# A GEGLU kernel in seven-product blocks: one unit's raw products set inside the unit before it, and a third weight sum handed to GpSimd

## The chip, the cores and the metric

The kernel runs on one core of a Trainium2 chip. The metric is the device time of one execution in microseconds (us), which is less when the kernel is better. The median of four runs of the kernel before is 543.22 us (543.09 to 543.28).

## What is computed

```python
def reference(x, w_gate, w_up, w_down):
    g = jnp.einsum("bsd,df->bsf", x, w_gate)
    u = jnp.einsum("bsd,df->bsf", x, w_up)
    h = _gelu(g) * u
    return jnp.einsum("bsf,fd->bsd", h, w_down)
```

x has 2048 rows of 1024, w_gate and w_up are 1024 by 3584, w_down is 3584 by 1024, all bf16; gelu is the tanh approximation.

## The kernel before, in words

**Passes and units.** The 2048 rows go in two passes of 1024. A pass holds its rows transposed in SBUF as `xT[c]`, c = 0 and 1, each 512 rows wide and cut into eight blocks of 128 along the contraction (ko = 0 to 7). The 3584 columns of w_gate and w_up go in 14 units of 256 columns (two blocks of 128). After the units of a pass comes the down projection (`down`), which the change does not touch.

**A unit.** Except for unit 0 of pass 0, each unit computes, for gate and for up (i = 0 and 1), a 2 by 2 block product with seven block products in place of eight (Winograd's form). The weight tile gives the blocks a11, a12 (first 128 columns, lower and upper half of the contraction), a21, a22 (second 128 columns). The sums of weights (`sums_s`, L151) are s1 = a21+a22, s2 = s1-a11, s3 = a11-a21, s4 = a12-s2, and sa, which is a22 cast by ScalarE; each name stands for two instructions, one for gate and one for up. The sums of x (`sums_t`, L136) are t1, t2, t3, t4 and the cast tb, each of four instructions, made once in a pass. The sums are fp32r tiles in the slots of one pool. Each product is four matmuls of 512 columns for gate and four for up, eight in all. `unit` (L193) issues them in this order: the raw bf16 products a11 (`first_product`, L188, snapped from its banks as `p1` by ScalarE; normally issued near the end of the unit before) and a12 (L205); then s2 times t2 on top of the a11 banks; s1 times t1 (into the banks `d`, snapped as `p5`); s3 times t3; s4 times tb; the next unit's a11; sa times t4. VectorE adds the parts (`add`, L196; L230, L231, L236) and multiplies gelu by up (`times`, L181); ScalarE does the gelu and the snaps. In a steady unit each of VectorE's operations takes one operand from PSUM and one from SBUF; the sums s and t of unit 1 are made from SBUF alone.

**Who makes the sums.** From unit 2 on, GpSimd makes a unit's weight sums one unit ahead (`make_s(ahead, pool)`, L524, in `prepare`, which `unit` calls as `after_p5` at L227). For unit 1, the first in seven-product form, VectorE makes all of s1 to s4, and t1 to t4.

**The start.** Unit 0 of pass 0 is computed plainly by `plain` (L471): with ko in pairs, four banks (gate and up, two column blocks) get eight matmuls each, first for c = 0 in `bank[0:4]`, then for c = 1 in `bank[4:8]`; `finish` (L486) does gelu and `times`. The rows of c = 0 are loaded and turned by TensorE (`turn`, L441); those of c = 1 come by eight transposing DMAs, one for each ko, in SyncE's queue (L468, L448). Unit 1's weights are loaded from ScalarE's queue (L497), unit 2's from ScalarE's queue inside unit 1 (`aside(-1)`, L204 and L541), and later ones by SyncE in `prepare` (L526), as soon as one of the three buffers of the pool `w` is free.

**What sets the order.** On SyncE, VectorE, GpSimd and TensorE the order of instructions is the order of the code (`manual_schedule(engines=ORDER)`, L67). On ScalarE it is planned by the framework, except in the start block (L492 to L507), where it is the code's order too. All semaphores are set by the framework from the tiles that an instruction reads and writes. In the start block the order is: warm-up, turning, unit 1's weight load, plain c = 0, t1, finish c = 0, s1, s2, t2, t3, tb, s3, sa, plain c = 1, finish c = 1. Then unit 1 issues its a11 products, its a12 products and so on; s4 and t4 are made in `aside(0)` (L542 to L544), after s2 times t2 has been issued.

Of the kernel before, what the change touches and what calls it, by code (L numbers as in the profile page):

```python
# [1 line left out]

# [8 lines left out]
def kernel(  # L11
# [23 lines left out]
    nc = tc.nc  # L35
    ENG = mybir.EngineType
# [14 lines left out]
    NKB = Dm // P  # L51
# [43 lines left out]
    def new(eng, a, b, op, name, shape=None, dtype=None):  # L95
        t = slot(shape or [P, N], dtype or f32r, name)
        eng(t, a, b, op)
        return t
# [15 lines left out]

    def load_w(u, queue=nc.sync, pinned=False):
        f0 = u * 2 * P
        w = wpool.tile([P, 2, NKB, 2 * P], bf16, name="w")
        for i, src in enumerate((w_gate, w_up)):  # L120
            got = queue.dma_start(
                out=w[:, i],
                in_=src[:, f0 : f0 + 2 * P].rearrange("(ko ki) f -> ki ko f", ki=P),
            )
            if queue is not nc.sync and not pinned:
                tc.keep_in_program_order(got)
        return w

    class Sums(dict):
# [6 lines left out]
    def sums_t(xT):  # L136
        K = range(KH)
        lo, hi = [[xT[c][:, k] for k in K] for c in range(2)], [
            [xT[c][:, KH + k] for k in K] for c in range(2)
        ]  # L140
        return Sums(
            how={
                "t1": lambda q: [new(dve, lo[1][k], lo[0][k], SUB, "t1") for k in K],
                "t2": lambda q: [new(dve, hi[1][k], q["t1"][k], SUB, "t2") for k in K],
                "t3": lambda q: [new(dve, hi[1][k], lo[1][k], SUB, "t3") for k in K],
                "t4": lambda q: [new(dve, hi[0][k], q["t2"][k], SUB, "t4") for k in K],
                "tb": lambda q: [cast(hi[1][k], "tb") for k in K],
            }
        )

    def sums_s(w, eng):  # L151
        GU = range(2)
        sh = [P, KH, P]
        a11, a21 = [[w[:, i, :KH, h : h + P] for i in GU] for h in (0, P)]
        a12, a22 = [[w[:, i, KH:, h : h + P] for i in GU] for h in (0, P)]
        return Sums(
            how={
                "s1": lambda q: [new(eng, a21[i], a22[i], ADD, "s1", sh) for i in GU],
                "s2": lambda q: [new(eng, q["s1"][i], a11[i], SUB, "s2", sh) for i in GU],
                "s3": lambda q: [new(eng, a11[i], a21[i], SUB, "s3", sh) for i in GU],  # L160
                "s4": lambda q: [new(eng, a12[i], q["s2"][i], SUB, "s4", sh) for i in GU],
                "sa": lambda q: [cast(a22[i], "sa", sh) for i in GU],
            }
        )

    def make_t(xT):
        t = sums_t(xT)
# [16 lines left out]
    def product(ps, lhs, rhs, start):  # L184
        for k in range(KH):
            matmul(ps, lhs[:, k, :], rhs[k], start and k == 0, k == KH - 1)
# [6 lines left out]
    def unit(u, banks, xT, w, s, t, p1, after_p5, aside, keep, ahead_of_p4, snap_first):  # L193
        GU = range(2)

        def add(ps, other):  # L196

            g = new(dve, ps[0], other[0], ADD, "sum", dtype=f32)
            dve(ps[1], ps[1], other[1], ADD)
            return g, ps[1]  # L200

        b21 = [xT[0][:, KH + k, :] for k in range(KH)]
        e, c, d = banks
        aside(-1)  # L204
        for i in GU:  # L205
            product(c[i], w[:, i, KH:, :P], b21, True)
        g, up = add(c, p1)
        for i in GU:
            product(e[i], s["s2"][i], t["t2"], False)
        aside(0)  # L210
        keep(0, c[0])
        if snap_first:
            with tc.manual_schedule(engines={ENG.Activation}):
                u2 = [snap(e[i], "u2") for i in GU]
                g = gelu(g)
        else:
            g = gelu(g)
        times(2 * u, 0, g, up)
        if not snap_first:
            u2 = [snap(e[i], "u2") for i in GU]  # L220
        keep(1, c[0])
        keep(2, c[1])
        c = d
        for i in GU:
            product(c[i], s["s1"][i], t["t1"], True)
        p5 = [snap(c[i], "p5") for i in GU]
        after_p5()  # L227
        for i in GU:
            product(e[i], s["s3"][i], t["t3"], False)
        g, up = new(dve, e[0], p5[0], ADD, "sum", dtype=f32), banks[1][1]  # L230
        dve(up, e[1], p5[1], ADD)  # L231
        for i in GU:
            product(c[i], s["s4"][i], t["tb"], False)
        times(2 * u + 1, 1, gelu(g), up)
        aside(1)
        g, up = add(c, u2)  # L236
        ahead_of_p4()
        for i in GU:
            product(e[i], s["sa"][i], t["t4"], False)
        times(2 * u, 1, gelu(g), up)  # L240
        aside(2)
        times(2 * u + 1, 0, gelu(e[0]), e[1])
# [222 lines left out]
    wf = wpool.tile([P, 2, NKB, 2 * P], bf16, name="w")  # L465
    for k0, k1 in ((0, 2), (2, 5), (5, NKB)):
        load_wf(nc.sync, k0, k1)
    for ko in range(NKB):  # L468
        transposing(xT, 1, ko, N)

    def plain(ps, c, kos, parts=1):  # L471
        n = N // parts
# [15 lines left out]
            times(j, c, gelu(ps[2 * j]), ps[2 * j + 1])  # L488

    on_dve, on_act = nc.vector.tensor_copy, nc.scalar.copy  # L490
    t = sums_t(xT)
    with tc.manual_schedule(engines={ENG.Activation}):  # L492
        for _ in range(NWARM):
            nc.tensor.matmul(bank[3], lhsT=warm[:, :P], rhs=warm, start=True, stop=True)
        for i in range(NS):
            turn(xT, xn0, 0, i, on_act if i == 1 else on_dve)
        w = load_w(1, nc.scalar, pinned=True)  # L497
        s = sums_s(w, dve)
        plain(bank[0:4], 0, range(0, 2), parts=2)
        plain(bank[0:4], 0, range(2, NKB))  # L500
        t.make("t1")
        finish(bank[0:4], 0)
        s.make("s1", "s2")
        t.make("t2", "t3", "tb")
        s.make("s3", "sa")
        plain(bank[4:8], 1, range(NKB))
        finish(bank[4:8], 1)  # L507

    def making(u):
        if u < 2 or u >= NU:  # L510
            return []
        return list(range(u - 2, NJ if u == NU - 1 else u - 1))

    nxt = {}
    ahead = None
    for ip in range(NPASS):
        for u in range(1 if ip == 0 else 0, NU):
            js = making(u) if ip == 0 else []

            def prepare():  # L520
                nonlocal ahead
                nxt["w"], nxt["s"] = ahead, None
                if u + 1 < NU:
                    nxt["s"] = make_s(ahead, pool)  # L524
                if u + 2 < NU:
                    ahead = load_w(u + 2)  # L526
                if len(js) == 1:
                    store_made(js[0])
                for j in js[1:]:
                    keep_whole(j)  # L530
                if ip == 0:
                    fetch_wd(making(u + 1))

            def keep(part, ps):
                if js:
                    keep_part(js[0], part, ps)

            def aside(part):
                nonlocal ahead
                if ahead is None:  # L540
                    ahead = load_w(2, nc.scalar)  # L541
                if part == 0 and "s4" not in s:  # L542
                    s.make("s4")
                    t.make("t4")  # L544

            def ahead_of_p4():
                if u + 1 < NU:
                    nxt["p1"] = first_product(even if u % 2 else odd, xT, nxt["w"])

            e = odd if u % 2 else even  # L550
            p1 = nxt.pop("p1", None) or first_product(e, xT, w)
            unit(u, (e, cc, dd), xT, w, s, t, p1, prepare, aside, keep, ahead_of_p4, ip == 0 and u == 1)
            if u + 1 < NU:
                w, s = nxt["w"], nxt["s"]

        last = ip == NPASS - 1
        got, nxt = {}, {}

        def more(step):

            nonlocal ahead
            if last:
                return
            if step in (-1, 0, 2):
                store_made({-1: NJ - 3, 0: NJ - 2, 2: NJ - 1}[step])
            if step == 0:
                xT[:] = new_x()
            if step >= 24 and step % 2 == 0 and step // 2 - 12 < len(moves):
                c, ko = moves[step // 2 - 12]
                transposing(xT, c, ko, (2 * (ip + 1) + c) * N)  # L570
            if step == 50:
                got["w"], ahead = load_w(0), load_w(1)
            if step == 58:
                got["s"] = make_s(got["w"], dve)
            if step == 62:
                got["t"] = make_t(xT)

        down(ip, even + cc, dd + odd, last, more)
        even, odd, cc, dd = odd, even, dd, cc
        if not last:  # L580
            w, t, s = got["w"], got["t"], got["s"]
# [29 lines left out]
```

## Time and profile before

| | us |
|---|---|
| median of four runs | 543.22 |
| the profiled execution | 543.19 |
| its span | 541.1 |
| around the span | 2.1 |
| TensorE matmul busy | 534.9 (99%) |
| VectorE busy | 341.4 (63%) |
| ScalarE busy | 258.2 (48%) |
| GpSimd busy | 236.4 (44%) |
| TensorE's share of the chain that ended last | 96% |

The span is the time from the first to the last instruction in the profile of one execution. A row of the timeline merges neighbouring instructions of one group: its first number is the start, its second the busy time, xN the number of them, and the bracket the idle time before the first, with what ended it. Matmuls overlap (each row of one says 0.379 us for a bf16 matmul of 512 columns, while the next starts earlier), so a row's count and time must be read together to find how far apart they start. PE is TensorE, PEld its weight load, DVE VectorE, ACT ScalarE, POOL GpSimd, SP SyncE; SPq is SyncE's queue of DMA issues.

### The profile page before, as it was taken

To read this page: it belongs to the slowest core of one execution; us is meant where nothing else is said; L and a number is where in the kernel's file an instruction comes from. 1 tells how busy PE (TensorE), PEld (TensorE's weight loads), DVE (VectorE), ACT (ScalarE), POOL (GpSimd) and SP (SyncE) were. 2 spreads that over 40 slices of the span, in tenths; PEclk is the share of its full clock that TensorE was granted. 3 is DMA by queue.
4 is the path that set the end of the run, shared out by engine and by line. 5 is a ranking of instruction groups with operands and counts; after the bars stand their busy time and mean duration, and the time that the engine had idled before them with its cause. 6 is when DMAs were issued, how large, how long until landed. Compare 5 with 4: busy or idle time off the path is not lost.

```text
span 541.1 us, 7420 instructions
## 1 busy us (share of the span) xinstructions
PE 534.9 (99%) x2405; PEld 377.7 (70%) x2405; DVE 341.4 (63%) x526; ACT 258.2 (48%) x463; POOL 236.4 (44%) x212
## 2 busy tenths in 40 slices
PE   8999999999999999999999999999999999999997
PEld 4477777766776646888876677667777775488885
DVE  3886666676667895594945545555544459676730
ACT  2566666556665410255355555555555541114431
POOL 0069966677774400000097777777766600000000
PEclk9999999999999999999999999999999999999999
DMA  8875666666654899989772222222331069473751
GB/s 218 176 190 176 175 176 197 204 184 189 201 174 162 269 380 317 294 189 300 229 194 79 78 79 78 79 78 80 85 100 50 1 174 379 166 236 95 238 181 48
DMA packets 108133, 93.28 MB, mean 172 GB/s; under 512 B 17216, under 2 KB 92992, under 8 KB 108096
## 3 DMA queue, kind: packets, MB, share of 16 engines
q1 hardware_dynamic: 103936, 90.72, 57.6%
q10 hardware_dynamic: 4160, 2.10, 1.5%
q8 instruction: 19, 0.31, 0.2%
q14 instruction: 18, 0.15, 0.1%
HBM read 74.45 MB, written 15.20 MB: 166 GB/s over the span
## 4 chain that ended last, share of the span: by engine, by line
PE 96%; SPq 2%; DMA 2%; ACT 0%; issue 0%
PE bank L111 96%; SPq L448 2%; DMA xT<-in_x_dram 1%; DMA xn<-in_x_dram 1%; SPq L437 0%; ACT st L408 0%
## 5 line engine op out<-in xcount | busy, mean ns | idle before, releaser
L93 POOL TENSOR_TENSOR s<-w 128x512 fp32r<-128x512 bf16 x100 | 117.3, 1194 | 185.6 <-PE bank L111 155.1
L111 PE MATMUL bank<-t,s 128*128 128x512 f32 x648 | 157.0, 398 | 0.0
L111 PEld LDWEIGHTS bank<-t,s 128*128 128x128 f32 x648 | 121.7, 188 | 27.7
L111 PE MATMUL bank<-xT,w 128*128 128x512 bf16 (+1 forms) x504 | 116.6, 377 | 0.3 <-DMA xT<-in_x_dram 0.2
L107 ACT COPY p<-bank 128x512 f32<-128x512 f32 x124 | 70.3, 591 | 92.2 <-PE bank L111 92.2
L90 DVE TENSOR_TENSOR hT<-g,bank 128x512 bf16<-128x512 f32 x112 | 76.6, 687 | 54.7 <-ACT g L178 48.3
L111 PEld LDWEIGHTS <-w 128*128 128x128 bf16 x504 | 45.0, 98 | 59.9 <-issue 14.3
L90 DVE TENSOR_TENSOR sum<-bank,p 128x512 f32<-128x512 f32 x54 | 37.4, 692 | 52.9 <-PE bank L111 51.2
L178 ACT ACTIVATE g<-sum 128x512 f32<-128x512 f32 x81 | 51.5, 636 | 33.3 <-DVE sum L90 32.3
L111 PE MATMUL bank<-q 128*128 128x512 f32 x240 | 58.9, 389 | 0.0
L111 PE MATMUL bank<-t,sa 128*128 128x512 f32 x216 | 58.6, 413 | 0.0
L93 POOL TENSOR_TENSOR s<-w,s 128x512 fp32r<-128x512 bf16 x50 | 57.7, 1177 | 0.0
L93 POOL TENSOR_TENSOR s<-s,w 128x512 fp32r<-128x512 f32 x50 | 57.1, 1163 | 0.0
L111 PE MATMUL bank<-tb,s 128*128 128x512 f32 x216 | 53.3, 389 | 0.0
L111 PEld LDWEIGHTS bank<-q 128*128 128x128 f32 x240 | 45.0, 188 | 9.4
L111 PE MATMUL bank<-raw,hT 128*128 128x512 bf16 x224 | 48.7, 379 | 0.0
L111 PEld LDWEIGHTS bank<-t,sa 128*128 128x128 f32 x216 | 40.7, 188 | 10.6
L111 PEld LDWEIGHTS bank<-tb,s 128*128 128x128 f32 x216 | 40.5, 188 | 8.4
L102 ACT CAST tb<-raw 128x512 fp32r<-128x512 bf16 x28 | 17.2, 626 | 60.0 <-PE bank L111 25.5
L107 ACT COPY u<-bank 128x512 f32<-128x512 f32 x62 | 35.9, 590 | 20.2 <-PE bank L111 20.2
L90 DVE TENSOR_TENSOR bank<-bank,p 128x512 f32<-128x512 f32 x54 | 37.8, 700 | 8.3 <-PE bank L111 5.2
L90 DVE TENSOR_TENSOR q<-hT 128x512 fp32r<-128x512 bf16 x56 | 38.5, 687 | 4.6 <-PE bank L111 4.6
(44 smaller groups left out, 441.0 us busy)
## 6 DMA issues: line engine op xcount, KB each, us to landing
raw<-in_w_down_dram SPq DMA_DIRECT2D x80, 256.0 KB, 4.8
q<-td SPq DMA_DIRECT2D x60, 256.0 KB, 4.9
w<-in_w_gate_dram SPq DMA_DIRECT2D x25, 512.0 KB, 5.5
w<-in_w_up_dram SPq DMA_DIRECT2D x25, 512.0 KB, 6.6
td<-m SPq DMA_DIRECT2D x12, 768.0 KB, 4.5
w<-td SPq DMA_DIRECT2D x6, 1024.0 KB, 9.7
out_dram<-st SPq DMA_DIRECT2D x32, 128.0 KB, 1.7
td<-w SPq DMA_DIRECT2D x2, 768.0 KB, 7.0
```

Of the source, the lines that this page charges most:

```text
L90: nc.vector.tensor_tensor(out=out, in0=a, in1=b, op=op)
L93: nc.gpsimd.tensor_tensor(out=out, in0=a, in1=b, op=op)
L102: nc.scalar.copy(out=t, in_=src)
L107: nc.scalar.copy(out=t, in_=ps)
L111: nc.tensor.matmul(ps, lhsT=lhs, rhs=rhs, start=start, stop=stop, skip_group_check=True)
L178: nc.scalar.activation(g, src, ACT.Gelu_apprx_tanh)
L448: nc.sync.dma_start_transpose(out=xT[c][:, ko, :], in_=x2[r0 : r0 + N, ko * P : (ko + 1) * P])
```

## The change

Five edits, all in pass 0 around units 0 to 2.

1. Loads: unit 1's weights are loaded from SyncE's queue between the fourth and the fifth transposing DMA, unit 2's from the same queue after the eighth. No load is issued by ScalarE any more.
2. Order on TensorE: plain c = 1 is cut in two. After its first half (ko 0 to 3) come unit 1's a11 products and its a12 products, then its second half (ko 4 to 7), called from inside `unit` as `aside(-2)`.
3. Order on VectorE: t1, finish c = 0, s1, s2, t2, the sum of a12 and a11 (`add`), t3[0] and t3[1], finish c = 1, t3[2] and t3[3], s4, t4. s3 is not VectorE's any more.
4. GpSimd makes unit 1's s3: s3 of gate behind t2's last instruction, s3 of up behind t3[1]. The gate is a copy by GpSimd of one column of the tile that VectorE has just written (`pool_behind`). Unit 2's sums are gated in the same way behind t4's last instruction.
5. In unit 1 ScalarE's order is the code's order; the multiplication of the first quarter (`c11`) moves behind the sum with p5, and that sum's up part goes to the other bank of `cc`.

```diff
-    def load_w(u, queue=nc.sync, pinned=False):
+    def load_w(u, queue=nc.sync):
...
-                "t3": lambda q: [new(dve, hi[1][k], lo[1][k], SUB, "t3") for k in K],
+                "t3": lambda q, K=K: [new(dve, hi[1][k], lo[1][k], SUB, "t3") for k in K],
...
-                "s3": lambda q: [new(eng, a11[i], a21[i], SUB, "s3", sh) for i in GU],
+                "s3": lambda q, GU=GU: [new(eng, a11[i], a21[i], SUB, "s3", sh) for i in GU],
...
+    def pool_behind(tile):
+        nc.gpsimd.tensor_copy(out=seen, in_=tile[:, :1].bitcast(f32))
...
         e, c, d = banks
-        aside(-1)
         for i in GU:
             product(c[i], w[:, i, KH:, :P], b21, True)
+        aside(-2)
         g, up = add(c, p1)
+        aside(-1)
         for i in GU:
             product(e[i], s["s2"][i], t["t2"], False)
         aside(0)
         keep(0, c[0])
         if snap_first:
-            with tc.manual_schedule(engines={ENG.Activation}):
-                u2 = [snap(e[i], "u2") for i in GU]
-                g = gelu(g)
+            u2 = [snap(e[i], "u2") for i in GU]
+            g = gelu(g)
         else:
             g = gelu(g)
-        times(2 * u, 0, g, up)
+        c11 = g, up
         if not snap_first:
+            times(2 * u, 0, *c11)
             u2 = [snap(e[i], "u2") for i in GU]
...
-        g, up = new(dve, e[0], p5[0], ADD, "sum", dtype=f32), banks[1][1]
+        g, up = new(dve, e[0], p5[0], ADD, "sum", dtype=f32), banks[1][not snap_first]
         dve(up, e[1], p5[1], ADD)
+        if snap_first:
+            times(2 * u, 0, *c11)
...
-    for ko in range(NKB):
+    for ko in range(KH):
         transposing(xT, 1, ko, N)
+    w = load_w(1)
+    for ko in range(KH, NKB):
+        transposing(xT, 1, ko, N)
+    ahead = load_w(2)
...
-        w = load_w(1, nc.scalar, pinned=True)
-        s = sums_s(w, dve)
         plain(bank[0:4], 0, range(0, 2), parts=2)
         plain(bank[0:4], 0, range(2, NKB))
         t.make("t1")
         finish(bank[0:4], 0)
+        plain(bank[4:8], 1, range(KH))
         s.make("s1", "s2")
-        t.make("t2", "t3", "tb")
-        s.make("s3", "sa")
-        plain(bank[4:8], 1, range(NKB))
-        finish(bank[4:8], 1)
+        nxt = {"p1": first_product(odd, xT, w)}
+
+    seen = xpool.tile([P, 1], f32, name="seen")
+    on_pool = sums_s(w, pool)["how"]["s3"]
+
+    def rest_of_0(part):
+        if part == 0:
+            t.make("t2", "tb")
+            plain(bank[4:8], 1, range(KH, NKB))
+            pool_behind(t["t2"][-1])
+            s["s3"] = on_pool(s, range(1))
+        else:
+            t3 = t["how"]["t3"](t, range(0, 2))
+            pool_behind(t3[-1])
+            s["s3"] += on_pool(s, range(1, 2))
+            finish(bank[4:8], 1)
+            t["t3"] = t3 + t["how"]["t3"](t, range(2, KH))
+            s.make("sa")
...
             def prepare():
                 nonlocal ahead
+                if first:
+                    pool_behind(t["t4"][-1])
...
             def aside(part):
-                nonlocal ahead
-                if ahead is None:
-                    ahead = load_w(2, nc.scalar)
+                if (ip, u) == (0, 1) and part < 0:
+                    rest_of_0(part + 2)
                 if part == 0 and "s4" not in s:
                     s.make("s4")
                     t.make("t4")
...
-            unit(u, (e, cc, dd), xT, w, s, t, p1, prepare, aside, keep, ahead_of_p4, ip == 0 and u == 1)
+            first = (ip, u) == (0, 1)
+            with tc.manual_schedule(engines={ENG.Activation}) if first else nullcontext():
+                unit(u, (e, cc, dd), xT, w, s, t, p1, prepare, aside, keep, ahead_of_p4, first)
```

## The prediction

> **What bounds the kernel now.** I read the chain of waits first, then TensorE's timeline at the start, the busy table by stretches, and last the timelines of VectorE and GpSimd where the change puts new work. Two lines of the chain (start, length, what):
>
> ```profile
> 15.52 4.89 DMA xT<-in_x_dram
> ...
> 20.45 517.16 PE bank L111 x2303
> ```
>
> From 20.45 us to the end the chain is TensorE alone. Before it stands SyncE's queue of transposing DMAs, whose last landing it waits for. The busy table gives, for one steady unit (length, then busy of PE, PEld, DVE, ACT, POOL):
>
> ```profile
> 37.83:50.43 12.60, 12.60 (x58) 8.93 (x57) 8.79 (x14) 8.00 (x15) 12.60 (x12) 1.00 0.55 169
> ...
> 276.67:289.27 12.60, 12.60 (x58) 8.92 (x57) 6.81 (x11) 6.84 (x12) 12.01 (x11) 1.00 0.65 166
> ```
>
> Units take 12.60 in both passes, at full clock, whatever the other engines do. A unit has 16 bf16 and 40 f32 matmuls; these start 0.216 and 0.227 apart, which makes 12.54, so nothing but two small steps between the types is left in it. Only the start has holes, in TensorE's timeline of 14 to 22 us:
>
> ```profile
> 13.78 5.99 PE L111 MATMUL bank<-xT,w 128*128 128x512 bf16 x27
> 19.97 2.36 PE L111 MATMUL bank<-xT,w 128*128 128x512 bf16 x9 [0.21 <-DMA xT<-in_x_dram]
> ```
>
> 27 matmuls of 0.379 each in 5.99 start 26 x 0.216 = 5.61 after the first: no hole. The last of them starts at 19.39, the next not at 19.61 but at 19.97: **0.36 lost**. The 9 after it span 2.36; without a hole they would span 8 x 0.216 + 0.379 = 2.11: **0.25 more**, within the same wait for the last two transposes. Together 0.62 (0.585 and 0.475 in place of 0.216 each). A third hole, 0.19 at 7.4 us (waiting for unit 0's up weights), is not touched. So the three holes, 0.81 us, bound whatever a reordering of the start can win; 0.2% of 543.22, about what a measurement of this kernel can tell from no change, is 1.09.
>
> **Edit 2, TensorE's order.** No matmul is added or removed. Plain c = 1 starts at 13.78 + 3 x 0.216 = 14.43. Its first 16 end at 17.88; a11 runs to 19.61, a12 to 21.34, the second half (ko 4, 5 from 21.34, ko 6, 7 from 23.07) to 24.6, where f32 begins (25.22 now). If all inputs are there: minus 0.62, and every later point is 0.62 earlier: s3·t3 (17th f32) at 28.43, s4·tb at 30.89 - 0.62 = 30.27, sa·t4 at 34.25 - 0.62 = 33.63.
>
> **Edit 1, the loads.** SyncE's issues now:
>
> ```profile
> 5.96 10.81 SPq L448 DMA_TRANSPOSE xT<-in_x_dram  x8
> ```
>
> The transposes are 1.30 apart; the fourth ends at 11.56. Gate and up of unit 1 (0.5 each) then issue at 11.6 and 12.1 (now on ScalarE, 10.81 and 11.41), transposes 5 to 8 at 12.65 to 16.56 (1.05 later than now), unit 2's weights at 17.85. Unit 1's two loads now land 4.3 and 6.0 after issue: 15.9 and 18.1, against a need of TensorE at 17.88 and 18.75. The last transpose takes 4.9 now, the longest of those I looked at 5.9, the shortest 2.9: 19.5 to 22.5, I take 21.5; ko 7 is first needed at 23.3. All in time: 0, with 0.6 of cover on up. Without cover: the longest landing of such a load in the trace is 8.8 (unit 2's up; it stood behind 1.5 MB of other loads, this one behind 0.64 MB). Below nothing: no, the cover only grows. Unit 2's weights arrive some 8 us earlier than at present (31.36 in GpSimd's row). Unit 3's load waits for unit 0's buffer, released at 24.8 in place of 22.15; behind it in SyncE's queue stand two raw loads for ScalarE at 38.22. With 5.9 to land from 26 they are there by 32: 0.
>
> **Edit 3, VectorE.** Now:
>
> ```profile
> 17.17 1.29 DVE L90 TENSOR_TENSOR s<-w 128x512 fp32r<-128x512 bf16 x2
> 18.37 1.29 DVE L90 TENSOR_TENSOR s<-s,w 128x512 fp32r<-128x512 f32 x2
> 19.57 2.49 DVE L90 TENSOR_TENSOR t<-xT,t 128x512 fp32r<-128x512 bf16 x4
> 21.98 2.50 DVE L90 TENSOR_TENSOR t<-xT 128x512 fp32r<-128x512 bf16 x4
> ```
>
> One operation every 0.60 in all these rows. After: s1 of up at 18.1 (landing), s2 18.7 and 19.3, t2 19.9 to 22.4, the a11+a12 sum 22.3 to 23.5, t3[0], t3[1] to 24.8. Finish c = 1 follows two gelus: their banks end at 23.7 and 24.5, 0.6 each, so VectorE multiplies at 24.7 and 25.3. Then t3[2], t3[3] to 27.2, s4 to 28.4, t4 to 30.8 (31.7 now). Needs: t2 at 24.6, t3 at 28.43, s4 at 30.27, t4 at 33.63. Slack 2.2, 1.2, 1.9, 2.8: all hidden, 0. With the longest landing (22.5) t2 ends 0.8 later and t3 still has 0.4. If cover were gone, each 0.1 over is 0.1 on the path. Taking s3 away (2 x 0.60) is what keeps t3 and s4 in time.
>
> **Edit 4, GpSimd.** The rows nearest to s3 beside VectorE:
>
> ```profile
> 31.36 1.34 POOL L93 TENSOR_TENSOR s<-w 128x512 fp32r<-128x512 bf16 x1 [30.06 <-DMA w<-in_w_gate_dram]
> ```
> ```profile
> 270.06 5.15 POOL L93 TENSOR_TENSOR s<-w 128x512 fp32r<-128x512 bf16 x2 [87.59 <-PE bank L111]
> ```
> ```profile
> 268.18 2.50 DVE L90 TENSOR_TENSOR t<-xT 128x512 fp32r<-128x512 bf16 x4
> 270.58 2.50 DVE L90 TENSOR_TENSOR t<-xT,t 128x512 fp32r<-128x512 bf16 x4
> ```
>
> Undisturbed a sum takes 1.16. Beginning beside VectorE's run on SBUF operands, the first took about 4.0 and ended 1.1 after VectorE's run (273.1), while VectorE kept its 0.60 pace: GpSimd simply waited. Beside operations with a PSUM operand (177.67 to 181.3 and each steady unit) both keep their pace. So s3 must begin inside a stretch of PSUM operations: gate's in 22.3 to 23.5, up's in 24.7 to 25.9. GpSimd's copy is in no row; bounds 0.10 (its 128x1 memset) and 1.34 (its slowest sum beside the tail of one VectorE operation); it handles one column, so I take 0.1, plus 0.2 for the two semaphores, an estimate. Then s3 of gate is 22.7 to 23.9, of up 25.1 to 26.3, needed at 28.43 and 29.34: hidden. Each laps 0.4 over VectorE's next SBUF operation; whichever waits, t3 still makes 28.43. Behind the third gate stand unit 2's eight sums: they start at about 31.1 (31.36 now), the first s2 is made by 34.6 and wanted at 37.83 - 0.62 = 37.2: 0. Both ends of the copy's price stay in the range of cases below.
>
> A rule speaks against this edit. The Trainium skill (GPSIMD Engine Reference, section 2.1 Instruction dispatch) says that the first call of a freshly loaded GpSimd routine pays about 6 us of code loading that no profile instruction shows. The 31.36 row began as its data landed and ran 1.34, but after 30 us of idleness, so this trace cannot show whether such a load lay under it. By the rule's 6 us before s3 of gate, both sums would miss their windows and come after 30.8, and the sum would be +2.4 or more; by the row it is 0.
>
> **Edit 5.** ScalarE's order in unit 1: p1 by 20.2, tb by 23, the two gelus by 25.2, sa by 26.3, u2 by 27.6, the gelu, p5 by 29.4. s3·t3 needs u2 by 28.43, s4·tb needs p5 by 30.27: 0.
>
> **Sum.** 541.1 - 0.62 = 540.5 of span, plus 2.1 around it: 542.6 (the execution, 543.19, is 0.03 under the median, which gives 542.6 too).
>
> **Rivals.** (a) The hole moves: the new order puts VectorE's a11+a12 sum and the finish of c = 1 ahead of t3's second half and s4, and late landings or the lapping eat the 1.2 of slack. For: 0.4 is left with the slowest transpose. Against: all rows at hand leave some. Price 0.2 to 1.0 back: 542.8 to 543.6. (b) Slower: s3 of up misses its window. From t3[1]'s end (24.8) to t3[2]'s start (25.9) there is 1.1; if semaphore and copy take more, GpSimd waits, as at 270.06, for the end of eight SBUF operations at 30.8, makes s3 by 32.0 and TensorE, which wants it at 29.34, stands 2.7: +2.1, 545.3. For: the upper bound of the copy, 1.34. Against: the lower. (c) Unit 1's up lands 8.8 after issue, at 20.9: TensorE stands 2.1: +1.5, 544.7. (d) More than 1.09 won: the holes hold only 0.81, so it would have to come from outside the start.
>
> **Chances.** Forecast (542.3 to 542.8) 0.76; (a) 0.11; (b) 0.07; (c) 0.03; (d) 0.03. The range takes the forecast and (a): its low end is all three holes closed and 0.1 of spread between runs, 542.3, its high end that of (a), 543.6; 0.13 is left out. Faster by over 0.2%: (d), 0.03; slower by over 0.2%, (b) and (c), 0.10; within, 0.87.
>
> **What would show it.** Right: TensorE's bf16 rows run without a bracket from 7.30 on, the first f32 row starts at about 24.6, units stay at 12.60, and the chain is TensorE's from about 7 us. GpSimd has two sums of about 1.2 between 22 and 27. Wrong: an f32 row of unit 1 longer than 0.227 per matmul, with a wait for POOL or DVE named; an s3 row of 2 us or more; a bracket on the a11 row naming the weights' DMA.

## The result and the profile after

The changed kernel takes 542.28 us (median of 39 runs, 541.6 to 544.01), the kernel before 543.43 in the same comparison (57 runs). The ratio is 0.9976, 95% interval 0.9969 to 0.9984: faster by 0.24%. The gain in the medians, 1.15, is more than the 0.81 that the prediction held for the most a reordering of the start could win. The forecast of 542.6 was 0.3 too high and its range began at 542.3. One run of e9 below, which took 1955 us, and its trace are left out of what follows.

The gain has two parts that the profile keeps apart. The median span of the 39 runs is 540.5; before's median less what lies around its span (2.15 in the runs below) gives 541.28: **0.78 less inside the span** (0.6 to 1.2 when the runs are resampled). Around the span lie 1.80 in place of 2.15: **0.35 less outside it**.

Inside, TensorE's timeline of the changed kernel from 14 to 22 us, and from 22 on (start, busy time, count):

```profile
13.80 8.37 PE L111 MATMUL bank<-xT,w 128*128 128x512 bf16 x38
```
```profile
21.79 3.40 PE L111 MATMUL bank<-xT,w 128*128 128x512 bf16 x15
24.84 5.83 PE L111 MATMUL bank<-t,s 128*128 128x512 f32 x24
```

38 matmuls in 8.37 are 37 x 0.216 + 0.379: both brackets of before are gone. f32 begins at 24.84, where before had 25.22. TensorE's first plain product came 0.21 later in this execution (7.51 against 7.30), so from the first product to the first f32 it is 17.33 against 17.92, **0.59 less**, for 0.62 forecast. From there on nothing differs. In every trace but those of e7 and e8 (below), of the old order and the new, the span ends 515.78 to 515.84 after the first f32 product (515.83 in both of these), so the gain inside the span lies wholly ahead of it. Two stretches of a unit:

```profile
37.45:50.05 12.60, 12.60 (x58) 8.92 (x57) 8.56 (x14) 8.06 (x15) 12.60 (x12) 1.00 0.50 162
276.29:288.89 12.60, 12.60 (x58) 8.93 (x57) 6.81 (x11) 6.84 (x12) 12.01 (x11) 1.00 0.65 166
```

One is of each pass, 12.60 as before. The chain now starts from unit 0's weights and not from the transposes:

```profile
3.07 4.83 DMA w<-in_w_up_dram
...
7.95 529.28 PE bank L111 x2366
```

VectorE, and then GpSimd, where the new work stands:

```profile
18.87 0.69 DVE L90 TENSOR_TENSOR s<-w 128x512 fp32r<-128x512 bf16 x1 [2.12 <-DMA w<-in_w_up_dram]
...
24.29 1.40 DVE L90 TENSOR_TENSOR t<-xT 128x512 fp32r<-128x512 bf16 x2
25.61 1.27 DVE L90 TENSOR_TENSOR hT<-g,bank 128x512 bf16<-128x512 f32 x2
26.80 1.47 DVE L90 TENSOR_TENSOR t<-xT 128x512 fp32r<-128x512 bf16 x2
28.19 1.28 DVE L90 TENSOR_TENSOR s<-w,s 128x512 fp32r<-128x512 bf16 x2
29.40 2.49 DVE L90 TENSOR_TENSOR t<-xT,t 128x512 fp32r<-128x512 bf16 x4
```
```profile
23.24 0.18 POOL L165 COPY seen<-t 128x1 f32<-128x1 f32 x1 [21.93 <-DVE t L90]
23.38 1.16 POOL L93 TENSOR_TENSOR s<-w 128x512 fp32r<-128x512 bf16 x1
25.82 0.18 POOL L165 COPY seen<-t 128x1 f32<-128x1 f32 x1 [1.29 <-DVE t L90]
25.96 1.16 POOL L93 TENSOR_TENSOR s<-w 128x512 fp32r<-128x512 bf16 x1
32.02 0.18 POOL L165 COPY seen<-t 128x1 f32<-128x1 f32 x1 [4.90 <-DVE t L90]
```

Both s3 run their undisturbed 1.16 inside their windows. The price of the lapping is read from the pairs of t3: 1.40 and 1.47 in place of 1.29. All of VectorE is 0.7 to 1.1 later than forecast, because up of unit 1 landed at 18.87; t3 still ends at 28.27, before TensorE asks for it at 28.69.

### The profile page after: what moved, and what is told of

The parts are those of the page before. It is cut to its first block, busy times and chain, and to the rows that moved or that the text cites. A ratio compares the mean times of both kernels' runs of the same rounds, so it can differ in the third digit from the quotient of the medians.

```text
span 540.7 us, 7419 instructions
## 1 busy us (share of the span) xinstructions
PE 534.9 (99%) x2405; PEld 377.9 (70%) x2405; DVE 340.9 (63%) x524; ACT 258.4 (48%) x463; POOL 239.0 (44%) x217
## 4 chain that ended last, share of the span: by engine, by line
PE 98%; DMA 1%; SPq 0%; ACT 0%; issue 0%
PE bank L111 98%; DMA w<-in_w_up_dram 1%; SPq L441 0%; ACT st L412 0%; SPq L458 0%
## 5 line engine op out<-in xcount | busy, mean ns | idle before, releaser
L93 POOL TENSOR_TENSOR s<-w 128x512 fp32r<-128x512 bf16 x102 | 119.4, 1190 | 154.6 <-PE bank L111 154.6
```

Of the source, the lines that this page charges most:

```text
L93: nc.gpsimd.tensor_tensor(out=out, in0=a, in1=b, op=op)
```

## The experiments

Theory 1: the gain inside the span is the wait for the last transposes, and that wait differs from one execution to the next. Theory 2: the 0.35 outside comes with the queue that issues the loads. Theory 3: unit 2's late weights cost something. All spans below are medians, beside before's measured along with them on the same chip; "around" is the time less the span. Most single spans of one kernel lie within 1 us of their median, so a difference of two medians under some 0.5 us says little by itself.

| | span | before's span | around | ratio to before (95%) |
|---|---|---|---|---|
| e1 loads from ScalarE | 540.0 | 541.5 | 1.80 | 0.9963 (0.9951 to 0.9975) |
| e2 loads from SyncE, old order | 542.3 | 541.5 | 2.16 | 1.0016 (1.0007 to 1.0024) |
| e3 no late transposes | 540.1 | 541.5 | 2.16 | 0.9977 (0.9967 to 0.9988) |
| e4 one small ScalarE load | 540.9 | 541.5 | 1.80 | 0.9987 (0.9977 to 0.9996) |
| e5 six more on ScalarE | 540.6 | 541.3 | 1.80 | 0.9980 (0.9966 to 0.9995) |
| e6 six more on VectorE | 540.6 | 541.3 | 1.94 | 0.9982 (0.9967 to 0.9997) |
| e7 s3 by VectorE | 540.75 | 541.3 | 2.04 | 0.9985 (0.9972 to 0.9998) |
| e8 no gate for unit 2 | 548.35 | 541.3 | 1.82 | 1.0115 (1.0093 to 1.0137) |
| e9 shorter VectorE code | 541.1 | 541.2 | 1.91 | 0.9982 (0.9954 to 1.0009) |
| e10 before again | 541.25 | 541.2 | 2.14 | 0.9983 (0.9958 to 1.0009) |
| e11 changed again | 540.35 | 541.2 | 1.78 | 0.9962 (0.9935 to 0.9988) |
| e12 e1 again | 540.4 | 541.2 | 1.81 | 0.9970 (0.9943 to 0.9997) |
| f1 changed, busy start | 540.6 | 541.6 | 1.79 | 0.9965 (0.9951 to 0.9979) |
| f2 before, busy start | 542.1 | 541.6 | 2.13 | 1.0004 (0.9993 to 1.0015) |
| f3 e9 again | 541.1 | 541.6 | 1.91 | 0.9983 (0.9971 to 0.9994) |
| f4 four more on VectorE | 540.65 | 541.6 | 2.18 | 0.9982 (0.9969 to 0.9995) |

Among e9 to e12 the unchanged kernel itself (e10) stands at 0.9983, since two of the runs of before beside it took 549 and 550 us; there the medians of the spans say more than the ratios.

### The hole: e3, e2, e10, f2, f3

e3 takes the wait away from the kernel before, without any of the change:

```diff
-                            xT[c][:, ko, cols],
+                            xT[c][:, ko % KH if c else ko, cols],
```

> The kernel before, but the plain products of c = 1 read the first four blocks of x twice in place of all eight, so that TensorE has nothing to wait for from the last transposes until t2 is used (unit 0's second half is computed from the wrong blocks). Loads as before. Theory 1: the two holes go, and the time shows what they cost in the mean: 0.9 to 1.3 us under before. If they cost the profiled 0.62 in every execution: 0.6 under before. Theory 2: 2.1 stays around the span. Theory 3: 0 to 0.3 under before.

Its span is 1.4 under before's, with the time around it unchanged (2.16): theory 1, just over the 0.9 to 1.3 expected. Resampled, the 1.4 is 0.5 to 1.8, so it does not by itself rule out the profiled 0.62. TensorE's timeline has no bracket (one matmul record is missing; 47 x 0.216 + 0.379 = 10.53):

```profile
13.77 10.52 PE L111 MATMUL bank<-xT,w 128*128 128x512 bf16 x47
```

e2 gives the kernel before edit 1 alone, and the third gate:

```diff
-    for ko in range(NKB):
+    for ko in range(KH):
+        transposing(xT, 1, ko, N)
+    w = load_w(1)
+    for ko in range(KH, NKB):
         transposing(xT, 1, ko, N)
+    ahead = load_w(2)
...
-        w = load_w(1, nc.scalar, pinned=True)
...
+                if (ip, u) == (0, 1):
+                    nc.gpsimd.tensor_copy(out=seen, in_=t["t4"][-1][:, :1].bitcast(f32))
```

> The kernel before with edit 1 alone (both loads from SyncE's queue) and the gate of GpSimd behind t4; TensorE's order as before. Theory 1: the hole before the last two plain products stays or grows, since the last four transposes issue 1.05 us later: 0 to 1.0 us over before. Theory 2: 0.3 us less around the span, so -0.3 to +0.7. Theory 3: 0.3 to 0.7 us under before.

The loads alone make it slower, by 0.8 in span: the later transposes land later and the old order waits for them. TensorE, 14 to 24 us:

```profile
13.76 4.05 PE L111 MATMUL bank<-xT,w 128*128 128x512 bf16 x18
19.19 5.17 PE L111 MATMUL bank<-xT,w 128*128 128x512 bf16 x21 [1.39 <-DMA xT<-in_x_dram]
```

The eighteenth starts at 13.76 + 17 x 0.216 = 17.43, the next at 19.19: 1.54 lost at one place, and 0.26 at the product after it. The new order is what makes room for the new place of the loads. Theory 3, which wanted 0.3 to 0.7 under before, falls, and so does theory 2: no load comes from ScalarE here and 2.16 lies around the span.

e10 is the kernel before once more, f2 the same with three more warm-up products while TensorE waits for x:

```diff
+            if i == 1:
+                for _ in range(3):
+                    nc.tensor.matmul(bank[3], lhsT=warm[:, :P], rhs=warm, start=True, stop=True)
```

> The kernel before once more, for a second trace and more spans on one chip beside the two below. If the hole were the same in every execution: 0.36 and 0.25 us lost at the last two plain products of c = 1, as in the first trace. Theory 1 (the hole changes with the landing of the last transposes against TensorE's start): another size, and a span that goes with it.

> The kernel before with the same three products. Theory 1 (its end hangs on the last transposes, so an earlier or faster start of TensorE only makes the hole longer): median span as before, 541.2 to 541.5, with a hole of 0.6 to 1.2 us in the trace. Rival (before also hangs on TensorE's start): median span 0.3 or more under before's.

The second trace of before (e10) loses 0.29 and 0.25 at the first products of c = 1 that read ko 6 and ko 7, 0.54 in all, and its span, 540.8, is 0.4 under the median. f3 (below; the start is that of before) loses 0.47 at ko 4 and 5 and 0.64 at ko 6 and 7, 1.11 in all. f2, whose order is the same, loses more in its trace, and at ko 4 already:

```profile
13.81 4.70 PE L111 MATMUL bank<-xT,w 128*128 128x512 bf16 x21
19.39 6.80 PE L111 MATMUL bank<-xT,w 128*128 128x512 bf16 x29 [0.88 <-DMA xT<-in_x_dram]
```

13.81 + 20 x 0.216 = 18.13, the next at 19.39: 1.05, and 0.16 after it. The transposing DMA of ko 4, issued at 11.61 in the first trace of before and at 11.46 in f2, lands 5.9 after issue there and 7.9 here, 17.56 and 19.34. Unit 1's weights are on their way at the same time, from the other queue. So the hole in the old order is 0.54, 0.62, 1.11 and 1.21 in four traces, and it follows the landing of the last four transposes. f2's span is 0.5 over before's where I expected none; the busier start won nothing, as theory 1 says, but whether it lost, and why, is not settled.

### TensorE's start: e1, e12, e4, e11, f1

e1 and e12 are the changed kernel with both loads put back into ScalarE's queue (edit 1 undone, the rest kept):

```diff
-    for ko in range(KH):
+    for ko in range(NKB):
         transposing(xT, 1, ko, N)
-    w = load_w(1)
-    for ko in range(KH, NKB):
-        transposing(xT, 1, ko, N)
-    ahead = load_w(2)
...
+        w = load_w(1, nc.scalar)
...
+        ahead = load_w(2, nc.scalar)
```

> The changed kernel with the loads of units 1 and 2 issued by ScalarE again and all eight transposes in a row; order on TensorE, VectorE and GpSimd as changed. Theory 1 (the whole gain is the wait for the last transposes, longer in the usual execution than the 0.62 us profiled): as fast as the changed kernel, 1.3 us under before. Theory 2 (0.3 us of the gain lies around the span, 2.1 against 1.8, and comes from issuing no load from ScalarE): span as changed, 2.1 around it, about 1.0 us under before. Theory 3 (unit 2's weights land so late in some executions that TensorE stands in unit 1): part of the gain lost, 0.6 us under before, and a wait of TensorE on those weights in some traces.

> The changed kernel with the loads of units 1 and 2 from ScalarE's queue once more, since only six runs of it were kept. If where the loads are issued is worth something: span 0.3 to 0.6 under the changed kernel's. Theory 1 (only the order on TensorE counts): as the changed kernel within 0.2.

e11 is the changed kernel once more:

> The changed kernel once more, on one chip with before: no hole between the second and the last plain product whenever TensorE starts; median span 0.6 to 1.1 us under before's, 1.8 around it.

e1's six runs looked better than the changed kernel; twelve more (e12, 540.4) stand level with it (e11, 540.35). Where the loads are issued is worth nothing measurable once the order is the new one, and e11's span is 0.85 under before's. Edit 2 carries the gain inside the span: it is what moves the first f32 product forward. Edits 3 and 5, which feed the new order, were not undone alone. Around e1 and e12 lie 1.8 although they load from ScalarE, which ends theory 2; e4 says the same:

```diff
+        nc.scalar.dma_start(out=extra, in_=x2[:P, :32])
```

> The changed kernel with one more load, 8 KB into a tile that nobody reads, issued by ScalarE after the turning. Theory 2: 2.1 around the span in place of 1.8, 0.3 us slower than the changed kernel, 1.0 under before. Theories 1 and 3: as the changed kernel, 1.3 us under before.

Of the 49 spans of e1, e4, e5, e12 and f4, 16 are 541.4 to 542.1, while most others lie at 540 to 541; of the 51 of the changed kernel and e11, 4 are 541.4 or more. The traces of these five were taken in such executions, and all show one thing; e8's shows it too. The 16 transposes by TensorE before the plain products, first in e12 and then in the changed kernel:

```profile
5.90 1.89 PE L448 MATMUL bank<-ident,xn 128*128 128x128 bf16 x16 [0.47 <-DMA xn<-in_x_dram]
7.58 1.70 PE L111 MATMUL bank<-xT,w 128*128 128x256 bf16 x7
```
```profile
6.35 1.33 PE L448 MATMUL bank<-ident,xn 128*128 128x128 bf16 x16 [0.91 <-DMA xn<-in_x_dram]
7.51 1.70 PE L111 MATMUL bank<-xT,w 128*128 128x256 bf16 x12
```

7 products in 1.70 against 12: they start 0.213 apart, not 0.109. In the six traces this lasts until 9.5 to 10.4 us and puts 0.7 to 1.1 us on the way from the first of them to the first f32; the traces of the spans under 541 (the changed kernel, e6, e7, e11, f1) have full rate from 4.9 to 7.2 us on. The granted clock in the rows reads 1.00 all the while; the spacing tells it. The Trainium skill (TensorE: Matmul & The Clock Gate, Part 1: The HAM clock gate) says that TensorE begins at half rate and is switched up after some 3.4 us of sustained work. In the trace of before the spacing halves at 4.5 us, 3.3 after the first warm-up product, which agrees. In the traces of the new order TensorE waits for x in that stretch, and the switch comes early or late. The bracketed wait is 0.47 to 1.10 in the six late ones and 0.16 to 0.91 in the five others, so its length does not decide alone; what does is open. f1 fills the wait in the changed kernel, with f2's diff:

> The changed kernel with three more warm-up products between the second and the third turning, where TensorE waits 0.5 to 1.2 us for x. Theory 1 (in the changed kernel the end hangs on TensorE's own start, and the late executions are those in which its products run at half rate until about 10.3 us): the upper spans, 541.4 and more, go; median span 540.0 to 540.4. Rival (the late executions have another cause): the spread stays, 539.8 to 542, and the three products are added, up to 0.5 us.

None of its nine spans is over 541.1 (f4, measured beside it, has four of ten over 541.4). But e11, without the three products, has none of twelve over 540.7, so this does not show that they did it; and f1's median, 540.6, is not the 540.0 to 540.4 expected, so it is no better version. None of the six traces in the old order had the late switch; I leave open whether that is chance.

### The 0.35 us around the span: e5, e6, f4, e9, f3

The trace records code loads too, without the engine they are for. The last one of 8 KB stands here (us from the span's start), beside the number of VectorE's instructions in the trace:

```
              VectorE   around   last 8 KB of code    end of span
changed           825     1.80   512.8                540.7
e5                825     1.80   513.3                541.6
f3 (as e9)        826     1.91   514.6                541.1
e7                827     2.04   542.6, after it      540.8
before            829     2.15   542.7, after it      541.1
f4                829     2.18   543.5, after it      541.8
e6                831     1.94   541.8, after it      540.7
```

e5 and e6 add six copies of one column to ScalarE's and to VectorE's code at the start, f4 four to VectorE's. This is e6's edit:

```diff
+        for _ in range(6):
+            on_dve(out=extra, in_=warm[:, :1])
```

> The changed kernel with six more copies of one column by ScalarE while it is idle at about 9 us. So far 1.8 us lies around the span of the changed kernel and its two variants, 2.15 around that of before and its two, and only the second three load 8 KB of code after the span's end. Theory A (ScalarE's code is that much longer in the second three, 688 or more instructions in the trace against 687 or fewer, and its tail fetches one more block): 2.15 around the span. Theory B (VectorE's code is, 829 against 825): 1.8. Span as the changed kernel's in both.

> The changed kernel with six more copies of one column by VectorE while it is idle at about 9 us. Theory A (ScalarE's length): 1.8 around the span. Theory B (VectorE's length): 2.15 around the span, 0.35 us slower than the changed kernel.

> The changed kernel with four more copies of one column by VectorE at about 9 us, which gives VectorE as many instructions as it has before (829). Theory B: a code load after the end, and 2.15 around the span if the place of the last block in the code decides; 1.9 to 2.0, as with six more, if only whether it is fetched. Span as the changed kernel's.

e9 and f3 take work from VectorE in the kernel before:

```diff
-        dve(t3, rr[:, 1, :], rr[:, 0, :], SUB)
+        (pool if j < 2 else dve)(t3, rr[:, 1, :], rr[:, 0, :], SUB)
```

> The kernel before, but in the down projection of each pass two of the fourteen sums of raw w_down blocks are made by GpSimd, which is idle there, so that VectorE's code has four instructions fewer (825 if no semaphore instruction comes or goes). Theory B (0.35 us of the gain is a last block of VectorE's code, fetched after the span): 1.8 us around the span in place of 2.15, no code load after the end, span as before, so 0.35 us under before without any of the change. If the 0.35 has another cause: 2.15.

> The kernel before with two of the fourteen sums of raw blocks in each pass made by GpSimd, once more, for an undisturbed trace. Theory B (code of VectorE fetched after the span): 1.9 around the span as the first time, and if 0.35 belongs to the fetch alone, no code load after the end. If a code load still follows the end at 1.9, the time around the span depends on where the last block begins and not only on whether there is one.

f4 is the test that counts: the changed kernel with four idle instructions on VectorE, 829 as before, has 2.18 around its span and the code load after it, 0.38 of the gain given back without a clear change in the span. ScalarE's six do nothing. In the other direction f3, with 826, has no load after the end and 1.91. So the length of VectorE's code moves both the time around the span and the late load. That the late load is what costs the time is not shown: f3 without it (1.91) and e6 with it (1.94) stand level. Nor does the length alone decide: of e7's twelve runs, all of one program, eight have 2.03 to 2.13 around the span and four 1.73 to 1.80. Why 831 cost less than 829, and why 826 cost 0.1 with no late load, stays open too. The change has 825 because two s3 left VectorE (edit 4) and its code has two semaphore instructions fewer, 298 for 300. e7, with s3 back, has 298 too, so these two do not go with s3: the other edits took them.

### Edit 4: e7, e8

e7 gives s3 back to VectorE, between t3 and s4 (`s.make("s3")` after t3 in place of the two `pool_behind` and `on_pool`):

> The changed kernel with s3 made by VectorE, between t3 and s4, in place of GpSimd. In the changed trace t3 ends at 28.3 and s3 times t3 begins at 28.7: with 1.2 us more ahead of it TensorE would stand 0.2 to 0.4 us at s3, once. Theory 1 (the gain is the hole alone and edit 4 only keeps new waits away): span 0.2 to 0.4 over the changed kernel's, still 0.5 or more under before's. If edit 4 carries the gain: as before.

```profile
24.79 5.97 PE L111 MATMUL bank<-t,s 128*128 128x512 f32 x24
```

The 24 f32 products take 5.97 in place of 5.83: 0.14 of waiting. The medians of the spans are too scattered to show it, but the span ends 515.98 after the first f32 product, 0.15 more than in the other traces. That is what GpSimd's s3 is worth in TensorE's time; the 0.24 more around the span come on top.

e8 leaves out the third gate:

```diff
-                if first:
-                    pool_behind(t["t4"][-1])
```

> The changed kernel without the gate behind t4: GpSimd begins unit 2's sums as soon as s3 is made and the weights are there, at about 27 us, beside VectorE's run of t3, s4, t4 on SBUF operands. If GpSimd only waits for VectorE, as at 270 us in the trace before: span as the changed kernel's. If a running GpSimd sum makes VectorE wait: each one puts up to 1.2 us before s4 or t4, with 1.8 and 1.7 of slack there: 0 to 1 us over.

Both prices were far too small: the median span is 7.8 us over the changed kernel's. In the traces it is 7.68, of which 1.44 stand ahead of the first f32 product (26.28 against 24.84; e8's trace is one with the late switch) and 6.24 behind it, where the missing gate acts. GpSimd, VectorE and TensorE of e8:

```profile
26.62 4.32 POOL L93 TENSOR_TENSOR s<-w 128x512 fp32r<-128x512 bf16 x3
30.89 3.18 POOL L93 TENSOR_TENSOR s<-s,w 128x512 fp32r<-128x512 f32 x2
34.03 3.16 POOL L93 TENSOR_TENSOR s<-w 128x512 fp32r<-128x512 bf16 x2
```
```profile
29.83 3.23 DVE L90 TENSOR_TENSOR s<-w,s 128x512 fp32r<-128x512 bf16 x2
32.98 6.33 DVE L90 TENSOR_TENSOR t<-xT,t 128x512 fp32r<-128x512 bf16 x4
```
```profile
34.43 1.67 PE L111 MATMUL bank<-xT,w 128*128 128x512 bf16 x7
39.96 2.84 PE L111 MATMUL bank<-t,sa 128*128 128x512 f32 x8 [3.86 <-DVE sum L90]
```

VectorE's four t4 take 6.33 in place of 2.49, about 1.58 apart, and GpSimd's sums 1.58 apart in place of 1.12: the two take turns, one whole instruction each. t4 ends at 39.3 in place of 31.9, and the sum behind them in VectorE's queue keeps TensorE waiting for 3.86. After that wait TensorE needs 2.84 for 8 products (2.19 in the changed kernel), and the granted clock reads 0.64 between 39.96 and 44.00: the wait is followed by a slower stretch, some 1.6 us more by the time unit 2's f32 products begin. The Trainium skill (SBUF — State Buffer, Who interferes with whom) says that a VectorE instruction with two SBUF inputs and a GpSimd instruction that reads SBUF contend for a shared pair of ports, held for a whole instruction, and that the order of issue decides who waits; e8's turns of one instruction each agree. In the trace of before at 270 us the same pair behaved otherwise: GpSimd waited for four VectorE instructions on end.

## Why the prediction was wrong

**"Plus 2.1 around it": this step failed.** The span came out at the 540.5 that the sum gives; around it lie 1.80, and these 0.3 are the whole miss. The sum carried the time around the span over as a constant, but the change moved it: VectorE's code lost four instructions, two of them by edit 4, and f4, which puts four back, has 2.18. Rival (d) said that more than 1.09 would have to come from outside the start; some of it did, and 0.03 was too little for it.

**What bounds the kernel, and edit 2: right.** Units stay at 12.60; the two holes went and 0.59 was won in the traced execution, for 0.62.

**"So the three holes, 0.81 us, bound whatever a reordering of the start can win": no bound.** It took a wait for a landing from one execution as a constant. The old order loses 0.54, 0.62, 1.11 and 1.21 in four traces, and both traces of before itself come from spans at or under the median (541.1 and 540.8 against 541.2 to 541.6). In the medians the change wins 0.78 to 0.85 inside the span. That this is more than 0.62 is likely, but not clear of the spread. That the span hit 540.5 is in part luck: before's median span is 541.28 in place of 541.1, and the 0.16 more that was won makes up for nearly all of it.

**Edit 1: right in sum, by luck on the transposes, and tight on up.** SyncE's issues in the changed kernel:

```profile
6.32 5.46 SPq L452 DMA_TRANSPOSE xT<-in_x_dram  x4
...
13.07 6.86 SPq L452 DMA_TRANSPOSE xT<-in_x_dram  x4
```

The prediction took the transposes as 1.30 apart throughout. Behind the two weight loads, four of them took 6.86 to issue, and the last was issued at 18.67, not 16.56; in all ten traces with the loads in SyncE's queue it is 17.7 to 19.1. It landed 2.8 after issue, not 4.9, so 21.47 stands beside the 21.5 forecast: two errors that cancel. What holds up the issues is not settled. Up of unit 1 reached VectorE at 18.87, not 18.1, and TensorE's first up product started at 18.98: the 0.6 of cover was used up, and e11 and e6 lose 0.17 and 0.39 there. Rival (c), in small.

**Edit 3: right.** t3 ends at 28.27 (27.2 forecast), t4 at 31.9 (30.8); the slack took it. Rival (a) did not come: e7, with 1.2 us more on VectorE, loses 0.14.

**Edit 4: price right, worth missed.** The copy takes 0.18, each s3 1.16, and the lapping 0.1 to 0.2 of VectorE's time. Rival (b) did not come. Of 6 us of code loading nothing shows between the first copy and the first sum, which start 0.14 apart. I counted the third gate as a delay that costs nothing; without it the earlier weights of edit 1 would have cost the 6.2 us that e8's trace shows behind the first f32 product.

**Edit 5: right.** u2 ends at 27.66 and p5 at 29.48, for 27.6 and 29.4 forecast, and TensorE waits for neither.

## What to carry to other kernels

A wait for a landing that one trace shows is one draw: before it is used as a bound on what a reordering can win, look at the spread of the spans and ask which of two chains, here TensorE's start and the last transposes, ends last in the other executions. Loads that arrive earlier also let their consumers start earlier; look for what those then run beside, and gate them if two engines would take turns on SBUF. Differences of 0.1% in short reorderings should be read as span and rest apart, since four instructions on an idle engine moved the rest by 0.38 us here. And a forecast that comes out at a landing time should be checked in its parts, issue and flight: here both were off and the sum was right.

## What was not expected of the hardware

- VectorE's code length moves the time around the span: 825 instructions 1.78 to 1.82 us, 829 instructions 2.13 to 2.18, with 8 KB of code loaded 1.6 to 1.8 us after the span's end in the latter. It is not the number alone: 831 gave 1.94, and 827 gave 1.75 in some executions and 2.05 in others.
- The transposing DMA of one block took 5.9 us to land in one execution and 7.9 in another, with the same neighbours in the queues.
- Behind two weight loads in the same queue, four transposing DMAs took 6.86 us to issue, where eight without such loads took 10.81.
- TensorE's products started 0.213 apart until 9.5 to 10.4 us in six traces, and 0.109 apart from their first in five others of the same order, while the granted clock in the rows read 1.00.
- GpSimd and VectorE, both on SBUF operands, took turns at 1.58 us a pair in e8, while at 270 us in the trace before GpSimd got none for 2.9 us.
